# Batch 2 of a fused attention and MLP kernel put in the order of the later batches, and the loads and transposes of batches 3 and 4 moved to other places and queues

## The chip, the cores and the metric

The kernel runs on one core of one Trainium2 chip. The metric is the device time of one execution in microseconds (us); a lower time is better. A core has five engines that run side by side, each with its own queue of instructions in order: TensorE (PE in the profile; PEld are its weight loads), VectorE (DVE), ScalarE (ACT), GpSimd (POOL) and SyncE (SP), which here only issues DMAs. GpSimd issues DMAs too, between its own instructions. All share 16 DMA engines.

## The reference

Eight batches of eight heads with 576 tokens and a head width of 64 go through causal attention with a forgetting gate; the result, laid out as tokens by 512 features, goes through a two-layer MLP (512 to 2048, exact GELU, 2048 to 512). All data are given as fp32.

```
scores = scale * np.matmul(q, k.transpose(0, 1, 3, 2))
log_f = np.log(np.clip(f, 0.0001, 1.0))
cum = np.cumsum(log_f, axis=-1)
decay = cum[:, :, :, None] - cum[:, :, None, :]
scores = np.where(causal, -1000000000.0, scores + decay)
...
attn = attn / (np.sum(attn, axis=-1, keepdims=True) + 1e-09)
return np.matmul(attn, v).astype(np.float32)
...
h = x @ w_in
g = 0.5 * h * (1.0 + erf(h * inv_sqrt2))
return (g @ w_out).astype(np.float32)
```

## The kernel before

**Work of one batch.** The kernel goes through the batches one by one and writes the order of every engine's work out by hand. Heads are taken in four pairs `i`, the 576 tokens in five blocks of 128 (the last overlaps the fourth by 64). For each pair, `scores` makes four tiles `t` of transposed scores on TensorE (L319), ScalarE takes their exponential (L329), and GpSimd zeroes what lies above the diagonal with selects (L331), five for each pair. The decay of the forgetting gate is a weight on the keys: `weigh_v` multiplies v by it on GpSimd (L288) and writes the weight itself into a 65th column (L295). `attend` multiplies the exponentials with the weighted v (L350, "value products"); `divide` on VectorE divides by the 65th column (L369, L370) and leaves x. Then x has to be transposed into `xT`, which `x_dma` does with a DMA transpose from SP (L397). `gemm1` multiplies w_in with xT (L447, blocks `ffb` 0 to 15 of 128 hidden features), ScalarE applies GELU (L467), and the second product with w_out (L551 and others) gives 512 rows of the output, in four row blocks `ts`, copied and added by VectorE (L565, L575) and stored by SP (L579).

**The 64 tokens that are over.** 576 is 512 and 64. The MLP takes 512 tokens of each batch at a time; the last 64 tokens of all eight batches are collected in `tails` and go through the MLP together at the end. In batches 1 and 3 to 7, `attend` takes four query blocks, `tail` computes the 64 tokens for all heads in one go (L416), and `tail_end` transposes them into `tails` by DMA (L429). In batches 0 and 2, `blocks(b)` gives five blocks; in batch 2 the fifth block of xT is copied into `tails` by GpSimd (`x_tail`, L435) once xT is there.

**The filling.** While ScalarE works on a batch's exponentials, TensorE does the second product of the batch before: `take(fill, n)` puts n steps of it behind each score tile. A step marked "r" is two matmuls on 64 rows each, which write into two PSUM banks that VectorE adds up later (scores also use 64 rows); a step "n" is one matmul on 128 rows. `PLAN` is the order of the four row blocks with the PSUM pool ("o", "m" or "s") that holds each. Batch 2 has more to fill in: the second half of two row blocks of batch 0 (`gemm2_second`, 16 steps), the other two of batch 0 (`PLAN_0`, 32) and all of batch 1 (`PLAN_1`, 64); a later batch has the 64 of its predecessor.

**Order in batches 3 to 7** (`attention`). All score tiles with their filling; then the value products of pairs 0 to 3 (`av`, and `av_both` for pairs 1 and 2 together in a PSUM bank pair of scores), the tail between fills, the rest of the filling, and `gemm1_open`, which starts seven blocks of the first product in step with the arrival of x. VectorE then untangles q and k of the next batch (L269), sixteen copies for q and sixteen for k, and GpSimd weighs the next v.

**Order in batch 2.** The value products of pair i−1 come in the middle of the score tiles of pair i, with a divide and an x transpose each; those of the last pair come behind all scores. The first product has an opening of its own.

**What is loaded when.** There is one buffer for v (`v_sb`), one for the weighted v, and one for the transposed q and k (`tq_of`); q and k as loaded have two. So v of a batch can be loaded when the weighing of the batch before is over, and q, k can be transposed (`transpose_dma`, in two halves of four heads, L255) when the batch before is untangled. In batches 3 to 7 SP issues: the first half of q, k of the next batch, v of the next batch, the second half, and later x. In batch 2, SP issues x of pair 0, then v of batch 3 (L134) and the first half of q, k of batch 3, then x of the other pairs, and the second half behind them. GpSimd issues the load of q, k of batch b+2 (L120) among the weighings of batch b+1, at block 14 of the first product (block 9 in batch 1).

**A tile that is used twice.** x has four buffers; `tail_end` takes one of them as the fifth of a batch, so its divide waits until the x transpose of pair 0 is over. `behind` (L641) is a small GpSimd copy that makes GpSimd's queue wait until a tile is there; here it is used once, in batch 1.

Of the kernel before, what the change touches and what calls it, by code (L numbers as in the profile page):

```python
# [54 lines left out]
def kernel(  # L55
# [18 lines left out]
    XC = NBLK * P  # L74
    TL = S - TC
    assert B * TL == TC
# [281 lines left out]
    def normalize(b, i, h):  # L358
        if (b, i) not in x_of:
            x_of[b, i] = x_pool.tile([P, NBLK, 2, D], BF16, tag="x", name="x")  # L360
        nm = blocks(b)
        divide(x_of[b, i][:, 0:nm, h, :], o_of[b, i, h], nm)

    def blocks(b):
        return NBLK if b in (0, 2) else NBLK - 1
# [11 lines left out]
    def xT(b):  # L377
        if b not in xT_of:
            xT_of[b] = xT_pool.tile([P, n_dm, XC], BF16, tag="xT", name="xT")
        return xT_of[b]  # L380

    def to_xT(b, i, copy, pool=m_psum, tag="m", ps=None):
        if ps is None:
            shape = [P, 2, 1024] if pool is s_psum else [P, XC]
            ps = pool.tile(shape, BF16, tag=tag, name="ps_x")
            if pool is s_psum:
                ps = ps[:, 0, 0:XC]
        nm = blocks(b)
        for m in range(nm):
# [3 lines left out]
        copy(xT(b)[:, i, 0 : nm * P], ps[:, 0 : nm * P])  # L393

    def x_dma(b, i):
        nm = blocks(b)
        nc.sync.dma_start_transpose(  # L397
            xT(b)[:, i, 0 : nm * P].rearrange("d (m p) -> d m p", p=P),
            x_of[b, i][:, 0:nm].rearrange("p m h d -> p (m h d)"),
# [25 lines left out]
    def tail_end(b, o):  # L425
        x = x_pool.tile([P, NBLK, 2, D], BF16, tag="x", name="x")
        x = x.rearrange("p k h d -> p (k h) d")[:, 0:HP]
# [5 lines left out]

    def x_tail(b):
        nc.gpsimd.tensor_copy(tails[:, :, b], by_half(xT(b)[:, :, XC - TL :]))  # L435

# [40 lines left out]
    def gemm2(c):  # L477
# [43 lines left out]
    PLAN_0 = [(2, "o", 16 * "r"), (3, "m", 14 * "r" + 2 * "n")]  # L521
    PLAN_1 = [
        (0, "m", 14 * "r" + 2 * "n"),
        (1, "m", 14 * "r" + 2 * "n"),
        (2, "m", 12 * "r" + 4 * "n"),
        (3, "s", 16 * "n"),
    ]
# [3 lines left out]
    def gemm2_rows(c, plan):  # L531
# [4 lines left out]
        for ts, held, steps in plan:  # L536
            if held == "s":
                both = s_psum.tile([P, 2, d_model], FP32, tag="s", name="ps2")
                banks = [both[:, 0], both[:, 1]]
            else:  # L540
                pool = {"o": o_psum, "m": m_psum}[held]
                banks = [
                    pool.tile([P, d_model], FP32, tag=held, name="ps2")
                    for _ in range(2)
                ]
            ot = o_pool.tile([P, d_model], FP32, tag="ot", name="ot")
            for kt, step in enumerate(steps):
                last = kt == steps.rfind("r")
                for r in range(2 if step == "r" else 1):
# [5 lines left out]
                        start=kt == (steps.index("r") if r else 0),  # L555
# [546 lines left out]
```

## Time and profile before

| | |
|---|---|
| median of 3 runs | 330.33 us |
| lowest and highest | 328.84 and 330.5 us |
| profiled execution | 330.98 us |
| its span, first to last instruction | 329.3 us |
| TensorE, VectorE, ScalarE, GpSimd busy | 317.3, 179.6, 203.1, 131.2 us |
| DMA mean | 133 GB/s |
| first product, matmuls (L447) | 112.8 us, 379 ns mean of one |
| second product while filling (L551) | 104.4 us |

The span is a little shorter than the execution's time because what lies before the first and behind the last instruction is not in it. A matmul's own duration (379 ns) is longer than its share of the time, since matmuls overlap; a chain or a stretch tells better what a row of them takes. A timeline row has the start, the duration, the engine and line, the operation, what it writes and reads, the shape and the count; in brackets the idle time before it and what ended it. DMAs have two times: that of the issuing instruction on its queue, and that from the issue to the landing of the data.

### The profile page before, as it was taken

How to read it: one execution, taken by the hardware profiler on the slowest of the kernel's cores; microseconds unless marked ns; L12 is line 12 of the kernel's file. 1: busy time of each engine (PE TensorE's matmuls, PEld its weight loads, DVE VectorE, ACT ScalarE, POOL GpSimd, SP SyncE). 2: the span in 40 equal slices, each digit the busy share in tenths (PEclk: the TensorE clock that was granted, in tenths of full speed). 3: DMA queues.
4: the chain of work that ended last, by engine and by line, in shares of the span. 5: the costliest groups of instructions: out<-in, count | busy, mean ns of one | idle time of the engine just before them, and what ended most of it. 6: DMA issues, size and time to landing. Idle time of an engine off the chain costs nothing.

```text
span 329.3 us, 8075 instructions
## 1 busy us (share of the span) xinstructions
PE 317.3 (96%) x3291; PEld 168.9 (51%) x3323; DVE 179.6 (55%) x424; ACT 203.1 (62%) x296; POOL 131.2 (40%) x254
## 2 busy tenths in 40 slices
PE   7999799999999999999999999999999999999995
PEld 3664445445554456445644565455545564444443
DVE  5852566584458935792599449953795270010011
ACT  4896785984635797189808990899178936405600
POOL 8996883019426153804471356225512510000000
PEclk9999999999999999999999999999999999999999
DMA  7999999988998999499959794969610131021012
GB/s 114 190 192 211 207 189 124 185 176 144 196 220 180 146 201 199 74 158 170 218 76 175 141 222 95 176 120 202 129 41 3 66 82 56 0 88 42 0 47 83
DMA packets 94117, 43.93 MB, mean 133 GB/s; under 512 B 73344, under 2 KB 88960, under 8 KB 94080
## 3 DMA queue, kind: packets, MB, share of 16 engines
q1 hardware_dynamic: 76928, 26.90, 41.1%
q0 software_dynamic: 16752, 15.99, 30.8%
q8 instruction: 26, 0.43, 0.6%
q10 hardware_dynamic: 400, 0.52, 0.4%
q14 instruction: 11, 0.09, 0.1%
HBM read 36.85 MB, written 9.44 MB: 141 GB/s over the span
## 4 chain that ended last, share of the span: by engine, by line
PE 84%; DMA 9%; POOL 3%; issue 1%; ACT 1%; DVE 0%; another core or an unknown queue 0%; POOLq 0%; DVEq 0%
PE ps L447 35%; PE ps L551 26%; PE ps L491 8%; PE s L319 6%; PE o L350 5%; DMA q<-in_k_dram 3%; DMA k<-in_k_dram 3%; DMA v_sb<-in_v_dram 2%; DMA xT<-x 1%; PE o L416 1%; PE ps L615 1%; ACT e L329 1%; POOL q L120 1%; POOL k L120 1%; POOL v_sb L169 1%
## 5 line engine op out<-in xcount | busy, mean ns | idle before, releaser
L467 ACT ACTIVATE g<-ps 128x512 bf16<-128x512 f32 x138 | 75.8, 616 | 85.5 <-PE ps L447 84.4
L447 PE MATMUL ps<-xT,w_in_sb 128*128 128x512 bf16 x498 | 112.8, 379 | 1.9 <-remote 0.3
L551 PE MATMUL ps<-w_out_sb,g 64*128 64x512 bf16 (+1 forms) x737 | 104.4, 376 | 0.8 <-issue 0.5
L329 ACT ACTIVATE e<-s 128x896 bf16<-128x896 f32 x112 | 87.8, 836 | 15.3 <-PE s L319 13.8
L447 PEld LDWEIGHTS <-w_in_sb 128*128 128x128 bf16 x576 | 55.0, 98 | 67.1 <-issue 3.2
L331 POOL TENSOR_SCALAR_AFFINE_SELECT e<-e 128x256 bf16<-128x256 bf16 (+1 forms) x135 | 49.2, 386 | 86.5 <-ACT e L329 86.4
L551 PEld LDWEIGHTS <-g 64*128 64x128 bf16 (+1 forms) x751 | 42.1, 94 | 31.3 <-issue 1.3
L288 POOL TENSOR_TENSOR vw<-v_sb,wT 128x640 bf16<-128x640 f32 (+1 forms) x30 | 38.1, 1272 | 34.7 <-DMA v_sb<-in_v_dram 18.6
L269 DVE COPY qT<-tq 64x288 bf16<-64x288 bf16 x96 | 43.0, 448 | 2.9 <-DMA tq<-q 1.4
L565 DVE COPY ot<-ps 128x512 f32<-128x512 f32 x20 | 13.8, 692 | 54.3 <-PE ps L551 54.3
L319 PE MATMUL s<-qT,kT 64*128 64x256 bf16 (+1 forms) x336 | 37.8, 275 | 0.8 <-DVE kT L241 0.6
L269 DVE COPY kT<-tk 64x288 bf16<-64x288 bf16 x96 | 35.4, 369 | 3.8 <-DMA tk<-k 2.1
L500 DVE COPY ot<-ps 128x512 f32<-128x512 f32 (+2 forms) x9 | 5.7, 632 | 49.5 <-PE ps L491 49.5
L319 PEld LDWEIGHTS <-kT 64*128 64x128 bf16 x336 | 18.1, 94 | 19.8 <-issue 4.0
L491 PE MATMUL ps<-w_out_sb,g 128*128 128x512 bf16 (+2 forms) x142 | 27.9, 355 | 0.1
L370 DVE TENSOR_TENSOR x<-o,r 128x256 bf16<-128x256 f32 (+1 forms) x51 | 22.2, 435 | 4.9 <-DMA xT<-x 3.3
L350 PEld LDWEIGHTS <-e 128*128 128x128 bf16 x600 | 20.2, 98 | 4.6 <-issue 2.1
L350 PE MATMUL o<-vw,e 128*128 128x65 bf16 x600 | 21.4, 194 | 0.2 <-POOL e L331 0.2
L491 PEld LDWEIGHTS <-g 128*128 128x128 bf16 x144 | 13.5, 98 | 14.5
L575 DVE TENSOR_TENSOR ot<-ot,ps 128x512 f32<-128x512 f32 x27 | 18.6, 688 | 3.0 <-remote 0.7
L447 PE MATMUL ps<-tails,w_in_sb 128*128 128x512 bf16 x64 | 14.3, 378 | 0.0
L670 ACT ACTIVATE e<-s 128x1024 bf16<-128x1024 f32 (+1 forms) x13 | 12.1, 990 | 2.1 <-PE s L665 1.9
(92 smaller groups left out, 192.0 us busy)
## 6 DMA issues: line engine op xcount, KB each, us to landing
out_dram<-ot SPq DMA_DIRECT2D x32, 256.0 KB, 2.7
v_sb<-in_v_dram SPq DMA_DIRECT2D x24, 256.0 KB, 4.8
q<-in_q_dram POOLq DMA_DIRECT2D x6, 576.0 KB, 7.0
k<-in_k_dram POOLq DMA_DIRECT2D x6, 576.0 KB, 9.5
v_sb<-in_v_dram POOLq DMA_DIRECT2D x17, 128.0 KB, 6.3
w_in_sb<-in_moe_w_in_dram POOLq DMA_DIRECT2D x4, 512.0 KB, 8.3
w_out_sb<-in_moe_w_out_dram POOLq DMA_DIRECT2D x4, 512.0 KB, 8.5
v_sb<-in_v_dram SPq DMA_DIRECT2D x6, 128.0 KB, 4.6
```

Source lines behind the costliest of these rows:

```text
L269: nc.vector.tensor_copy(rows[:, odd], src[odd * D : (odd + 1) * D, 2 * i + h].rearrange("d j p -> d p j"),)
L288: eng.tensor_tensor(vw(b)[:, hs, n0:n1, 0:D], v_sb[:, hs, n0:n1, :], w.unsqueeze(3).to_broadcast([P, 2, n1 - n0, D]), Alu.mult,)
L319: nc.tensor.matmul(to, *ab, start=half < 0, stop=half == 1 or not masked)
L329: nc.scalar.activation(et[:, :, z:c], st[:, :, z:c], Act.Exp, scale=scale)
L331: nc.gpsimd.affine_select(out=et[:, :, c0 + z : c0 + P], in_=et[:, :, c0 + z : c0 + P], compare_op=Alu.is_ge, fill=0.0, base=z, pattern=[[ ...
L350: nc.tensor.matmul(o[:, m, :], e_of[b, i, t][:, h, c : c + P], vw_of[b][:, 2 * i + h, n, :], start=(n == 0), stop=(n == m),)
L370: nc.vector.tensor_tensor(x, o[:, 0:n, 0:D], r[:, 0:n].unsqueeze(2).to_broadcast([P, n, D]), Alu.mult,)
L447: nc.tensor.matmul(ps, w_in_sb[:, kt, ffb * P : (ffb + 1) * P], xT(c)[:, kt, 0:TC] if c < B else tails[:, kt % 2, :, kt // 2, :], start=(k ...
L467: nc.scalar.activation(g_of[c][ffb], ps, Act.Gelu)
L491: nc.tensor.matmul(pss[ts][:, c0:c1], g_of[c][kt][:, ts * P : (ts + 1) * P], w_out_sb[:, kt, c0:c1], start=(kt == 0), stop=(kt == n_ff - 1),)
L551: nc.tensor.matmul(banks[r], g_of[c][kt][rows, ts * P : (ts + 1) * P], w_out_sb[rows, kt, :], start=kt == (steps.index("r") if r else 0), ...
L575: nc.vector.tensor_tensor(ot, ot, bank, Alu.add)
```

## The change

Batch 2 goes through the same code as batches 3 to 7: four query blocks, all scores first, value products behind them, a tail, `gemm1_open`. `PLAN_1` and its special cases go, `PLAN_0` has 16 steps "r" in its second row block, and the counts of the filling for batch 2 change so that 101 of the 112 steps lie between its score tiles. `tail_end` has a tile of its own (tag "xt"), and xT shrinks from 640 to 512 columns. Both halves of q, k of batch 3 are transposed in the middle of batch 2's scores, ahead of every x. Behind the opening of batch 2's first product, GpSimd waits for the x of pair 3 (`behind`), loads v of batch 3, then q and k of batch 4, and only then weighs v of batch 3. In the batches behind it, `behind` stands in front of the load of q and k. The cut diff:

```diff
     def normalize(b, i, h):
...
-        nm = blocks(b)
-        divide(x_of[b, i][:, 0:nm, h, :], o_of[b, i, h], nm)
-
-    def blocks(b):
-        return NBLK if b in (0, 2) else NBLK - 1
+        divide(x_of[b, i][:, 0:NQ, h, :], o_of[b, i, h], NQ)
...
     def tail_end(b, o):
-        x = x_pool.tile([P, NBLK, 2, D], BF16, tag="x", name="x")
-        x = x.rearrange("p k h d -> p (k h) d")[:, 0:HP]
+        x = x_pool.tile([P, HP, D], BF16, tag="xt", name="xt")
...
-    def x_tail(b):
-        nc.gpsimd.tensor_copy(tails[:, :, b], by_half(xT(b)[:, :, XC - TL :]))
...
-    PLAN_0 = [(2, "o", 16 * "r"), (3, "m", 14 * "r" + 2 * "n")]
-    PLAN_1 = [
-        (0, "m", 14 * "r" + 2 * "n"),
-        (1, "m", 14 * "r" + 2 * "n"),
-        (2, "m", 12 * "r" + 4 * "n"),
-        (3, "s", 16 * "n"),
-    ]
+    PLAN_0 = [(2, "o", 16 * "r"), (3, "m", 16 * "r")]
...
         yield from gemm2_rows(0, PLAN_0)
-        yield from gemm2_rows(1, PLAN_1)
+        yield from gemm2_rows(1, PLAN)
...
-    FILL_2 = [[8, 8, 8, 8], [8, 8, 4, 4], [4, 4, 4, 4], [4, 4, 4, 4]]
+    FILL_2 = [[8, 8, 8, 8], [8, 8, 8, 7], [5, 5, 5, 5], [5, 5, 6, 2]]
...
         for i in range(HP):
             for t in range(4):
                 scores(b, i, t)
                 take(fill, counts[i][t])
-                if t == 1 and b == 2 and i > 0:
-                    av(i - 1)
-                    if i == 1:
-                        load_v(3)
...
-                if b > 2 and i == 0 and t == 1:
+                if b > 2 and (i, t) == (0, 1):
                     load_v(b + 1)
-                if b > 2 and t == 0 and i < 2:
-                    transpose_dma(b + 1, 4 * i, 4 * i + 4)
-                if b == 2 and t == 1 and i == 1:
-                    transpose_dma(3, 0, 4)
+                for half, at in enumerate([(2, 0), (2, 2)] if b == 2 else [(0, 0), (1, 0)]):
+                    if (i, t) == at:
+                        transpose_dma(b + 1, 4 * half, 4 * half + 4)
+        av(0)
+        av_both(b, 1)
+        av_both(b, 2)
+        av(3)
+        take(fill, 4)
+        tail_end(b, tail(b))
+        put_off.pop()()
+        take(fill, 999)
+        gemm1_open(b)
         if b == 2:
-            take(fill, 4)
-            transpose_dma(3, 4, 8)
-        take(fill, 999)
...
+            behind(xT(b), HP - 1)
+            load_v(b + 1, eng=nc.gpsimd)
+            load_qk_tokens(b + 2)
         if b + 1 < B:
             untangle(b + 1, 0)
             weigh_v(b + 1, 0)
-        if b == 2:
-            x_tail(b)
...
+                if ffb == (10 if b == 1 else 14) and b != 2 and b + 2 < B:
+                    if b > 2:
+                        behind(xT(b), HP - 1)
+                    load_qk_tokens(b + 2)
...
-                if ffb == (9 if b == 1 else 14):
-                    load_qk_tokens(b + 2)
```

## The prediction

> **What bounds the kernel now.** The first part of the page and the chain that ended last say it together.
>
> ```profile
> PE 317.3 (96%) x3291; PEld 168.9 (51%) x3323; DVE 179.6 (55%) x424; ACT 203.1 (62%) x296; POOL 131.2 (40%) x254
> PE 84%; DMA 9%; POOL 3%; issue 1%; ACT 1%; DVE 0%; another core or an unknown queue 0%; POOLq 0%; DVEq 0%
> ```
>
> TensorE is busy 96% of the span and is 84% of the chain; the DMA share lies in the first 45 us, before batch 2. So an edit pays only by taking work or gaps from TensorE. Next I cut the span into one stretch per batch, from its first score matmul to the next batch's (view of stretches; columns: length, then busy us and count of PE, PEld, DVE, ACT, POOL).
>
> ```profile
> 67.86:113.31 45.45, 44.87 (x427) 22.71 (x432) 30.08 (x66) 25.11 (x35) 22.24 (x41) 1.00 1.04 182
> 113.31:147.67 34.36, 33.91 (x347) 18.34 (x349) 23.25 (x56) 23.46 (x34) 14.69 (x30) 1.00 0.84 153
> 147.67:181.67 34.00, 33.84 (x347) 18.49 (x349) 23.56 (x54) 23.46 (x34) 14.76 (x30) 1.00 0.91 154
> ```
>
> Batch 2 takes 45.45 us, batch 4 takes 34.00, batch 3 34.36; the granted clock is 1.00 in all. Batch 2 is longer because it carries 112 filling steps of the second product (16 left of batch 0, 32, and 64 of batch 1) where a later batch carries 64. A step's price is in the chain view: 16 row-half matmuls of L551, eight steps, take 1.73 us, so 0.216 each. The 48 extra steps are 10.37 us, and batch 2 in a later batch's order should take 34.00 + 10.37 = 44.37 us. It takes 1.08 more. The PE timeline of batch 2 shows where.
>
> ```profile
> 79.16 0.38 PE L551 MATMUL ps<-w_out_sb,g 128*128 128x512 bf16 x1 [0.16 <-issue]
> 79.37 1.12 PE L350 MATMUL o<-vw,e 128*128 128x65 bf16 x30
> 80.42 0.36 PE L319 MATMUL s<-qT,kT 64*128 64x448 bf16 x2
> ```
>
> Between the row-half matmuls (64*128) and scores, each of three pairs' value products is cut in as full-height matmuls (128*128), with 0.16 us idle on the way in, at 79.16, 84.45 and 89.75.
>
> **TensorE's part, step by step.** (1) Value products go from five to four query blocks: 15 to 10 matmuls per head, 40 fewer; 30 take 0.95 us in the chain, so −1.27. (2) The tail is added: 40 matmuls of L416, 0.77 in batches 3 to 7. Net −0.50. (3) The three cut-ins go: −0.48 of shown idle. (4) The rest, 0.10, is the small loss on the way back to scores. The sum is −1.08, the same as the difference above. Steps "n" turned into "r" cost nothing: 35 full-height matmuls of L491 take 7.55 us, 0.216 each, a pair of row halves the same. The denser filling (8, then 5 steps between score tiles) leaves ScalarE more room than later batches' 3: five steps and a tile are 1.25 us, an exponential 0.84 (L329).
>
> **VectorE and PSUM.** Batch 2's 16 divides of five blocks (0.19 + 0.49) become those of batch 3 (eight of 0.18 + 0.42 turned partly into two pairs of 0.20 + 0.69, and a tail of 0.17 + 0.42), at the same or less work. An additional copy for the last row block (0.69) is hidden: VectorE waited 11.2 us for L551's matmuls in this batch. The o banks before the first value product are free in time by batch 3's row: copy ends 0.7 us and addition 1.5 us after the row block, while 1.2 us of matmuls and 0.33 of the first head lie between.
>
> **SP: v leaves, transposes move up.** Before, SP issues x of pair 0 at 81.93 (6.5 us to landing), then v of batch 3 for 7.13 us, and the second transposes (100.87 and 102.23) after x. Now the stores stay, the two q/k halves come in front of all x. They need k of batch 3: issued 76.28, landing 11.6 later, 87.9, with v and x beside it; less without. They take 1.3 to 2.2 us of SP each, so SP ends them near 93, and the third and fourth stores come behind (0.5 each). Value products start at 67.86 + (127.68 − 113.31) + 10.37 = 92.6; x of pair 0 is divided 1.7 later, 94.3. SP is free by then by under 1 us. I take 0 to 0.3 for this. The fifth transposition (tails by DMA, 1.2 us of SP at 135.68 in batch 3) replaces a GpSimd copy of 0.43 that waited 4.9 us for x; nobody needs tails until the end.
>
> **GpSimd and the DMA behind x.** x of pair 3 is issued 21.07 us after batch 3's start and lands 2.3 later; in batch 2 that is 67.86 + 10.37 + 23.4 = 101.6. Then the gate copy (0.19, row L641), five v issues (L134, 0.75 each: 3.75) and q, k (0.8 each) until 107.1. The last v issue, near 105, lands 4.3 to 6.9 later (POOL's v issues at 12.3 and 33.4; the second had other loads in front): 109 to 112, I take 110. The four weighings (1.28 + 0.27 each) then end near 116; before, they ended at 108. Behind them on GpSimd are batch 3's 20 selects (7.7 us). The next batch starts at 112.3, its value products at 126.7, the last at 128.7. So v may land as late as 128.7 − 6.2 − 7.7 = 114.8 before TensorE feels it: hidden, by 5 us. If that cover went, each us costs one. q, k of batch 4 are issued about when they were (104.98 before) and land near 115; in batches over 2 their gate waits for x of pair 3, which lands at 136.7 where q was issued at 136.35: 0.5 later, hidden by SP's wait for VectorE (transposes at 147.70).
>
> What is late next is the untangling on VectorE. These rows of batch 2 are of VectorE and of GpSimd:
>
> ```profile
> 101.47 3.53 DVE L269 COPY kT<-tk 64x288 bf16<-64x288 bf16 x4
> 102.02 1.33 POOL L288 TENSOR_TENSOR vw<-v_sb,wT 128x640 bf16<-128x640 f32 x1
> 105.03 3.37 DVE L269 COPY qT<-tq 64x288 bf16<-64x288 bf16 x4
> 105.79 0.77 POOL L120 DMA_DIRECT2D k<-in_k_dram  x1
> ```
>
> Four copies take 1.35 us alone and 3.5 beside GpSimd. From 102.02 to 108.1 VectorE lost 4.2 us to 6.1 us of GpSimd. Now GpSimd works 5.4 us issuing and 6.2 weighing under the same copies: about 7.5 lost at that row's two thirds (ends: nothing, and all 11.6). They start at 99.1 and end near 117.4, 5.1 us into batch 3 (1.9 before). First needed is pair 1 at +4.6, done by 110. But SP's transposes for batch 4 wait for these copies (113.93 after the last q copy), then load v (4.75), then the second half, two stores, and x of pair 0, issued 16.2 us into the batch. I reckon SP 0.9 us late there.
>
> ```profile
> 129.55 6.04 SPq L397 DMA_TRANSPOSE xT<-x x4
> 133.75 13.99 PE L447 MATMUL ps<-xT,w_in_sb 128*128 128x512 bf16 x63 [0.34 <-remote]
> ```
>
> In batch 3 that x took 4.1 us to land, and TensorE waited 0.34; in batch 4 it took 2.3 and nothing waited. SP late by 0.9 makes the wait 0 to 1.5; I take 0.6, 0.3 more than now.
>
> The load of q, k of batch 3, moved from block 9 to 10 of batch 1's first product, keeps its place on GpSimd between the weighings: nothing. The tail's own tile takes away VectorE's wait for x (3.3 us in three batches). TensorE did not wait for it: nothing.
>
> **Sum.** −1.1 + 0.1 (x in batch 2) + 0.3 = −0.7. The profiled execution took 330.98 us (span 329.3, 1.7 around it); it would become 330.3. The median of the runs, 330.33, is 0.65 lower, so I forecast 329.6.
>
> **A rule that speaks against it.** The row: q, k issued by GpSimd amid the copies took 0.82 and 0.77, as at 75.45 without copies (0.84, 0.77); VectorE's copies were what grew. The Trainium skill, "SBUF — State Buffer", section "SBUF: two separate sides", says that a VectorE copy in a two-port mode locks GpSimd out, so that descriptors of its DMAs can't be written; it names about 620 ns becoming 3100. By the row nothing is added; by the page's figure seven issues would last some 22 us, and v would come past its deadline.
>
> **Rivals.**
> (A) Forecast, 0.52: 329.6, own range 328.9 to 330.6.
> (B) All waits for x vanish in batches 2 and 3: −1.1 − 0.34, 328.9. For it: batch 4's 2.3 us. 0.18.
> (C) Slower: the chain GpSimd, VectorE copies, SP. x of pair 0 in batch 3 has 3.86 us from issue to need (129.55 to 133.41), against 2.3 to 4.1 of landing. Once SP is over 1.5 us late, each further us is TensorE's; at 4.5 late, with a landing of 2.3 to 3.2, it pays 3 to 3.9, net about +2: 332.3. For it: two thirds of the copies' slowdown is an estimate. Against: load v can wait less. 0.20.
> (D) GpSimd locked out until the copies end at 110: v's issues from 110 to 114, landing 118 to 121, weighings and selects 13.9 more: 132 to 135 against 128.7, and batch 4's transposes behind them: some 5 us, 335. This is what the page's rule would do; the row speaks against it. 0.05.
> (E) The transposes don't get in front as meant, because k of batch 3 lands late: x of batch 2 waits behind them by 1 us and takes the gain: 330.3. Against it: 87.9. 0.05.
>
> The range 328.6 to 332.0 leaves out D and most of C's end. Faster by over 0.5% (about what a measurement of this kernel can tell from no change; below 328.7): half of B and the low edge of A, 0.12. Slower (above 332): over half of C, and D, 0.17. Between: 0.71.
>
> **What would show it.** Right: batch 2 from first score to next near 44.4 us, no 0.16 idles inside; v landing by 112; weighings under the start of batch 3; first-product wait in batch 3 under 1 us. Wrong: a batch 3 over 35 us with an x landing as releaser, selects late at the value products, or a wait of L551 for a bank.

## The result and the profile after

| | before | after |
|---|---|---|
| median of 21 runs each | 330.11 us | 331.49 us |
| lowest and highest | 328.84 and 334.07 us | 330.43 and 334.54 us |
| ratio after to before, 95% interval | | 1.0051 [1.0028, 1.0075] |
| profiled execution, span | 330.98, 329.3 us | 332.16, 330.4 us |

The changed kernel is slower by about half a per cent. The forecast, 329.6, was a small gain. The time lies inside the range, on the side of rival C, but it moved the other way than was forecast.

These lines of the page of the changed kernel answer to the first two of before: busy time by engine, and the chain that ended last.

```profile
PE 321.0 (97%) x3338; PEld 169.8 (51%) x3338; DVE 178.8 (54%) x423; ACT 202.7 (61%) x296; POOL 136.6 (41%) x262
PE 91%; DMA 4%; DVE 2%; issue 1%; ACT 1%; POOL 1%; SPq 0%; POOLq 0%; DVEq 0%
```

They tell little: TensorE is still nearly always busy, with 3.7 us more of it, though the change gives it no more to do. Most of this is the record: the first profile of the kernel before has 3291 matmuls for 3323 weight loads, so 32 matmuls are missing from it, while a second profile (below) has all 3323 and 320.0 us. The 1.0 us that is left may go with the granted clock, which shows 0.6 in the second of the page's 40 slices, 8 to 16 us in, where the kernel before had 0.9 or more. The stretches by batch say more. The rows are batches 2, 3, 4, and batch 7 with the end (start and end, length, then busy us and count of PE, PEld, DVE, ACT, POOL, the granted clock, DMA share, GB/s).

```profile
68.12:112.58 44.46, 44.46 (x446) 22.14 (x446) 28.80 (x68) 24.58 (x35) 20.92 (x38) 1.00 0.84 168
112.58:148.34 35.76, 34.22 (x350) 18.40 (x351) 23.65 (x54) 23.47 (x34) 20.30 (x39) 1.00 0.91 165
148.34:182.34 34.00, 34.00 (x350) 18.49 (x350) 22.24 (x50) 23.47 (x34) 15.01 (x31) 1.00 0.81 153
250.34:330.40 80.06, 76.04 (x558) 38.12 (x557) 15.85 (x33) 33.62 (x51) 7.33 (x20) 1.00 0.16 48
```

The row of before for batch 7 and the end, not shown so far, is this one:

```profile
249.84:329.30 79.46, 75.61 (x553) 38.16 (x557) 15.96 (x33) 33.62 (x51) 7.33 (x20) 1.00 0.16 48
```

Batch 2 went from 45.45 to 44.46 us. (That all 44.46 are busy is no sign of a closed gap: in the second profile of the kernel before, all of batch 2's 45.45 are busy too.) Batch 3 went from 34.36 to 35.76; its POOL column grew by 5.6 us, since the weighings of v slid into it. Batch 7 with the end grew by 0.6. With the unrounded times (the spans are 329.27 and 330.45), from the first scores on: −0.98 (batch 2), +1.39 (batch 3), −0.17 (batch 6), +0.67 (batch 7 and end), in all +0.91; what lies before batch 2 adds 0.26. That is the difference between the spans. (What lies before batch 2 scattered by some 2 us between the profiles; from batch 2 on, the two of the kernel before agree within 0.02 us in every stretch, see below.)

**Batch 2** gained what was forecast. Its PE timeline where the value products come in, behind the last scores:

```profile
92.22 0.59 PE L530 MATMUL ps<-w_out_sb,g 64*128 64x512 bf16 x4
92.75 2.78 PE L350 MATMUL o<-vw,e 128*128 128x65 bf16 x80
95.37 1.02 PE L530 MATMUL ps<-w_out_sb,g 128*128 128x512 bf16 x4
96.32 0.84 PE L410 MATMUL o<-vw,e 128*64 128x65 bf16 x40
97.10 1.68 PE L530 MATMUL ps<-w_out_sb,g 128*128 128x512 bf16 x7
98.68 2.53 PE L437 MATMUL ps<-xT,w_in_sb 128*128 128x512 bf16 x11
```

The value products are one row of 80, then filling, the tail, filling, and the first product, whose x is there. No row carries an idle time in brackets. But the 0.16 that stood at each cut-in in the first profile of the kernel before were missing records and no idle time: the second profile has 14 matmuls in a row there, where the first has 12, a gap and 1.

```profile
76.88 2.00 PE L551 MATMUL ps<-w_out_sb,g 64*128 64x512 bf16 x14
78.72 1.12 PE L350 MATMUL o<-vw,e 128*128 128x65 bf16 x30
```

**Batch 3** pays. Its first product waits for x, 1.54 us. Before, it was 0.34 by the first profile, in which the matmul ahead of the wait is missing, and 0.13 by the second, which has it; the difference of 1.41 is all that batch 3 lost (1.39).

```profile
134.43 2.75 PE L437 MATMUL ps<-xT,w_in_sb 128*128 128x512 bf16 x12 [1.54 <-DMA xT<-x]
```

To see why that x is late, follow its queue, SP, back (timeline of SP; start and duration of the issue, not the landing):

```profile
115.29 1.28 SPq L255 DMA_TRANSPOSE tq<-q  x1
118.22 1.25 SPq L255 DMA_TRANSPOSE tk<-k  x1
119.57 4.80 SPq L134 DMA_DIRECT2D v_sb<-in_v_dram  x5
...
125.94 1.33 SPq L255 DMA_TRANSPOSE tq<-q  x1
127.33 1.62 SPq L255 DMA_TRANSPOSE tk<-k  x1
129.05 1.41 SPq L554 DMA_DIRECT2D out_dram<-ot  x2
130.65 6.45 SPq L391 DMA_TRANSPOSE xT<-x  x4
```

From 118.22 to 130.65 SP has hardly a gap. The kernel before in the same place:

```profile
115.40 1.50 SPq L255 DMA_TRANSPOSE tk<-k  x1
117.00 4.75 SPq L134 DMA_DIRECT2D v_sb<-in_v_dram  x5
...
125.97 2.23 SPq L579 DMA_DIRECT2D out_dram<-ot  x2
```

There the last store ends at 128.20 and x follows at 129.55: SP had 1.35 us to spare, until VectorE had divided x, 16.2 us into the batch. Counted from the batch's start, the transposition of k is issued at 5.64 instead of 2.09, 3.55 later; 1.35 of that is the spare time, 0.37 SP's shorter row of issues, and 1.83 is left: x is issued at 18.07 instead of 16.24. It lands 3.65 later and not 4.06, and TensorE needs it 20.31 into the batch: 18.07 + 3.65 − 20.31 = 1.41, and 0.13 from the landing to the matmul.

And why is k transposed late? Because it lands late, at 118.17, 0.05 before that issue. The timeline of GpSimd behind batch 2's first product:

```profile
101.83 0.34 POOL L616 CAST gate<-xT 96x1 f32<-96x1 bf16 x1 [8.17 <-DMA xT<-x]
102.35 4.56 POOL L134 DMA_DIRECT2D v_sb<-in_v_dram  x5 [0.19 <-issue]
106.91 0.85 POOL L120 DMA_DIRECT2D q<-in_q_dram  x1
107.75 0.86 POOL L120 DMA_DIRECT2D k<-in_k_dram  x1
113.16 1.28 POOL L288 TENSOR_TENSOR vw<-v_sb,wT 128x640 bf16<-128x640 f32 x1 [4.55 <-DMA v_sb<-in_v_dram]
```

The gate opens at 101.83, when x of pair 3 is there. The five v issues take 4.56 us, and v is complete at 113.0, 10.6 us after the first issue (the weighing at 113.16 waited for it). q and k stand behind v in the same queue: k, issued at 107.75, lands 10.4 us later, where before it took 8.6 from 105.79. VectorE is not what holds SP here; its untangling, from the first of these rows to the last, is over at 111.82:

```profile
99.42 1.33 DVE L269 COPY qT<-tq 64x288 bf16<-64x288 bf16 x4
...
110.48 1.34 DVE L269 COPY kT<-tk 64x288 bf16<-64x288 bf16 x4
```

### The profile page after: what moved, and what is told of

Same layout as the page of the kernel before. It is cut to its first block, busy times and chain, and to the rows that moved or that the text cites. A ratio compares the mean times of both kernels' runs of the same rounds, so it can differ in the third digit from the quotient of the medians.

```text
span 330.4 us, 8131 instructions
## 1 busy us (share of the span) xinstructions
PE 321.0 (97%) x3338; PEld 169.8 (51%) x3338; DVE 178.8 (54%) x423; ACT 202.7 (61%) x296; POOL 136.6 (41%) x262
## 4 chain that ended last, share of the span: by engine, by line
PE 91%; DMA 4%; DVE 2%; issue 1%; ACT 1%; POOL 1%; SPq 0%; POOLq 0%; DVEq 0%
PE ps L437 38%; PE ps L530 26%; PE ps L481 8%; PE s L319 6%; PE o L350 4%; DMA xT<-x 2%; PE s L640 2%; DMA q<-in_q_dram 2%; PE ps_f L226 1%; PE o L410 1%; PE ps L590 1%; ACT e L329 1%; PE o L671 1%; PE ps L566 1%; DVE x L366 0%
## 5 line engine op out<-in xcount | busy, mean ns | idle before, releaser
L530 PE MATMUL ps<-w_out_sb,g 64*128 64x512 bf16 (+1 forms) x766 | 107.1, 376 | 0.0
L269 DVE COPY qT<-tq 64x288 bf16<-64x288 bf16 x96 | 39.4, 410 | 2.5 <-DMA tq<-q 1.0
L269 DVE COPY kT<-tk 64x288 bf16<-64x288 bf16 x96 | 37.9, 394 | 3.6 <-DMA tk<-k 1.9
L550 DVE TENSOR_TENSOR ot<-ot,ps 128x512 f32<-128x512 f32 x28 | 19.3, 688 | 4.1 <-PE ps L530 2.1
L481 PEld LDWEIGHTS <-g 128*128 128x128 bf16 x144 | 13.5, 98 | 14.5
L350 PEld LDWEIGHTS <-e 128*128 128x128 bf16 x560 | 18.6, 98 | 3.9 <-issue 2.1
L350 PE MATMUL o<-vw,e 128*128 128x65 bf16 x560 | 19.7, 194 | 0.2 <-POOL e L331 0.2
L366 DVE TENSOR_TENSOR x<-o,r 128x256 bf16<-128x256 f32 x41 | 17.4, 424 | 1.4
```

Source lines behind the costliest of these rows:

```text
L269: nc.vector.tensor_copy(rows[:, odd], src[odd * D : (odd + 1) * D, 2 * i + h].rearrange("d j p -> d p j"),)
L350: nc.tensor.matmul(o[:, m, :], e_of[b, i, t][:, h, c : c + P], vw_of[b][:, 2 * i + h, n, :], start=(n == 0), stop=(n == m),)
L366: nc.vector.tensor_tensor(x, o[:, 0:n, 0:D], r[:, 0:n].unsqueeze(2).to_broadcast([P, n, D]), Alu.mult,)
L481: nc.tensor.matmul(pss[ts][:, c0:c1], g_of[c][kt][:, ts * P : (ts + 1) * P], w_out_sb[:, kt, c0:c1], start=(kt == 0), stop=(kt == n_ff - 1),)
L530: nc.tensor.matmul(banks[r], g_of[c][kt][rows, ts * P : (ts + 1) * P], w_out_sb[rows, kt, :], start=kt == 0, stop=last if r else kt == n_f ...
L550: nc.vector.tensor_tensor(ot, ot, bank, Alu.add)
```

## The experiments

The theory from these profiles: GpSimd's queue has v ahead of q and k of batch 4, so k lands late, SP's list of batch 4's transposes and loads starts late, and x of batch 3 stands at the end of that list. Rivals: the load of v of batch 4, which waits for the late weighings, is what holds SP; the order of batch 2's work is at fault by itself, or the moved loads by themselves; the gate (L616) holds GpSimd for nothing; the wait was a chance of that one execution. In the diffs, "-" is the changed kernel unless said otherwise. Ratios are to the kernel before.

**v of batch 3 earlier.** GpSimd loads it as soon as its buffer is free, amid batch 2's scores.

```diff
                     weigh_v(b, 3)
+                    load_v(3, eng=nc.gpsimd)
...
-            load_v(b + 1, eng=nc.gpsimd)
```

> v of batch 3 is loaded by GpSimd right behind the weighing of batch 2's v, about 20 us earlier; behind x only q, k of batch 4 are loaded. Theory S (the changed kernel loses in batch 3 because k of batch 4, queued behind v on GpSimd, lands at 118.2 where it landed at 114.4, so that SP transposes it late, loads v late and issues x of pair 0 late): k lands near 112, the wait before batch 3's first product falls from 1.5 us to 0.4 or less, batch 2 keeps its 44.5 us, and the whole is 1.0 us (0.6 to 1.6) faster than the kernel before. Rival G (the loss lies in the gates of the later batches or in the last batch): batch 3's wait goes, but the whole stays at or above the kernel before. Rival X (v now runs beside q, k of batch 3, which land later, and their transposes push x of batch 2): a wait of 1 us or more before batch 2's first product.

Measured: 1.0095 [1.006, 1.0131]. Batch 3 is mended, 34.76 us: k of batch 4 lands at 113.55, x of pair 0 is issued 16.25 us into batch 3, the wait is 0.54. But batch 2 takes 47.30. In the first row, from SP's timeline, a transpose of batch 3's first half lasts 4.35 us beside v's transfer; the second, from PE's, is TensorE's wait in batch 2, for an x that was issued only at 96.60 and landed at 99.68. (The row names a VectorE copy as releaser, but that is the last of several, long done.)

```profile
87.26 4.35 SPq L255 DMA_TRANSPOSE tk<-k  x1
```

```profile
99.81 13.97 PE L437 MATMUL ps<-xT,w_in_sb 128*128 128x512 bf16 x64 [2.73 <-DVE kT L269]
```

So the late v is the cause of batch 3's wait, and early v collides with the transposes that the change put in front of x.

**q, k of batch 4 ahead of v of batch 3** in GpSimd's queue.

```diff
-            load_v(b + 1, eng=nc.gpsimd)
             load_qk_tokens(b + 2)
+            load_v(b + 1, eng=nc.gpsimd)
```

> Behind x, GpSimd loads q, k of batch 4 first and v of batch 3 second. Theory S: k lands near 111, so the first transposes of batch 4 are on time, but v lands near 117 instead of 113, the weighing ends near 123 instead of 118.7, and SP, whose load of the next v waits for the weighing, is late by as much or more: the wait before batch 3's first product stays at 1.5 us or grows to 4, the whole is 0 to 2.5 us slower than the changed kernel. A rival by which only the landing of k counts: the wait falls to 0.4 or less and the whole comes to 1 us under the kernel before. A rival by which v's lateness reaches TensorE itself through the selects: a wait of the value products of batch 3 for GpSimd's selects or weighings.

Measured: 1.0149 [1.0114, 1.0184]. k lands at 111.62, as the theory wants, but v only at 116.23, and the weighings last to 122. Now v decides twice: selects behind the weighings come late for the value products, and SP's load of v of batch 4 waits for the weighings, to 121.97, so x is issued 20.85 us into the batch. Timeline of PE in batch 3:

```profile
128.50 1.00 PE L350 MATMUL o<-vw,e 128*128 128x65 bf16 x18 [0.61 <-POOL e L331]
...
135.18 5.12 PE L437 MATMUL ps<-xT,w_in_sb 128*128 128x512 bf16 x23 [2.42 <-DMA xT<-x]
```

The order in which the change issues them is the better one: what is too much behind the gate is the sum of both loads. In the changed kernel, too, v stands close behind k as a cause. The last of its weighing multiplications ends at 118.57, 1.0 us before SP, held by k, comes to the load of v of batch 4 (119.57), so a k on time would by itself have won back about 1 us of SP's time at most.

**v of batch 4 by ScalarE**, to take the load of 4.8 us out of SP's list.

```diff
-                if b > 2 and (i, t) == (0, 1):
+                if b > 3 and (i, t) == (0, 1):
                     load_v(b + 1)
+                if b == 3 and (i, t) == (2, 0):
+                    load_v(b + 1, eng=nc.scalar)
```

> The loads stay as in the changed kernel, but in batch 3 the five loads of batch 4's v are issued by ScalarE behind the scores of pair 2 instead of by SP. Theory S (SP's queue is what is late): SP issues x of pair 0 near 128.3 instead of 130.65, the wait before the first product of batch 3 falls from 1.5 to 0.4 us or less, the whole is 0.7 to 1.2 us faster than the kernel before. Rival D (the transfers themselves are late, not SP): x is issued on time and still lands past 133, the wait stays over 1 us. Rival A (ScalarE's five issues delay its exponentials): TensorE waits for exponentials in batch 3 by up to 3 us.

Measured: 1.0287 [1.0239, 1.0334]. The five issues held ScalarE for 7.76 us, the exponentials behind them came late, and TensorE waited 6.77 us in the midst of the scores (timeline of ScalarE):

```profile
119.73 7.76 ACTq L134 DMA_DIRECT2D v_sb<-in_v_dram  x5
127.54 2.21 ACT L329 ACTIVATE e<-s 128x768 bf16<-128x768 f32 x3 [7.25 <-DMA v_sb<-in_v_dram]
```

Within that wait the granted clock fell to 0.5, from 126.3 to 133.2, which adds to the time. The run says nothing on SP, because a larger wait lies in front of it.

**No gate** ahead of v.

```diff
-            behind(xT(b), HP - 1)
             load_v(b + 1, eng=nc.gpsimd)
```

> In batch 2 GpSimd no longer waits for x of pair 3 before it loads v of batch 3 and q, k of batch 4: v is issued from 94 on instead of 102. Theory S: v lands near 103, k of batch 4 near 110, the wait in batch 3 falls to 0.4 or less, and the whole is 0.5 to 1.2 us faster than the kernel before, less what x of batch 2 loses. Rival X (x shares the DMA engines with v): x of batch 2 lands 1 to 3 us later and the wait moves into batch 2, so the whole stays where the changed kernel is.

Measured: 1.0207 [1.0165, 1.0249]. Batch 3 is at 34.74 with a wait of 0.52, but batch 2 takes 52.31: v, issued from 92.6 on, runs beside the x transposes, which then land at 100.0, 104.6, 107.4 and 109.8, and the first product stands still four times (2.52, 1.79, 0.94 and 0.74 us). The first two, in the timeline of PE:

```profile
100.13 2.72 PE L437 MATMUL ps<-xT,w_in_sb 128*128 128x512 bf16 x6 [2.52 <-DMA xT<-x]
104.64 1.89 PE L437 MATMUL ps<-xT,w_in_sb 128*128 128x512 bf16 x8 [1.79 <-DMA xT<-x]
```

These waits are 5.99 of the 7.84 us that batch 2 takes longer than in the changed kernel; part of the rest is the granted clock, 0.5 from 99.7 to 103.1. The gate earns far more than it costs.

**The order of the work alone**: batch 2 in the new order, every load and transpose where it was before (cut; "-" is the changed kernel).

```diff
-            behind(xT(b), HP - 1)
-            load_v(b + 1, eng=nc.gpsimd)
-            load_qk_tokens(b + 2)
...
+                if b == 2 and (i, t) == (1, 1):
+                    load_v(3)
+                    transpose_dma(3, 0, 4)
...
         put_off.pop()()
+        if b == 2:
+            transpose_dma(3, 4, 8)
```

> One half of the change alone: batch 2 in the order of the later batches, but v of batch 3 and the first half of q, k of batch 3 issued by SP in the middle of batch 2's scores as in the kernel before, the second half behind x, and q, k of batch 4 loaded at block 14 behind three weighings. Theory S (the order is worth 1 us, the moved loads take it back in batch 3): batch 2 takes 44.4 to 45.1 us, batch 3 34.0 to 34.5, the whole is 0.5 to 1.2 us faster than the kernel before. Rival X (v and the transposes on SP make x of batch 2 late, which is what the moved loads were for): a wait of 1 to 3 us before batch 2's first product, and a whole at or above the kernel before.

**The loads and transposes alone**: batch 2 in the old order, with v by GpSimd, the gate and the transposes as in the change (cut; "-" is the kernel before).

```diff
-                    if i == 1:
-                        load_v(3)
...
-                if b == 2 and t == 1 and i == 1:
-                    transpose_dma(3, 0, 4)
+                if b == 2 and i == 2 and t in (0, 2):
+                    transpose_dma(3, 2 * t, 2 * t + 4)
...
-            transpose_dma(3, 4, 8)
...
+            behind(xT(b), HP - 1)
+            load_v(3, eng=nc.gpsimd)
+            load_qk_tokens(4)
```

> The other half alone: batch 2 in its old order, with both transposes of q, k of batch 3 in the middle of the scores, and GpSimd loading v of batch 3 and then q, k of batch 4 behind x of pair 3, ahead of weighing. Theory S: batch 2 keeps 45.4 us, batch 3 has the changed kernel's wait of 1 to 2 us before its first product, the whole is 0.8 to 1.8 us slower than the kernel before. Rival O (the loss comes with the new order, not with the loads): batch 3 near 34.4 us and the whole within 0.4 us of the kernel before.

Measured: order alone 1.0152 [1.0112, 1.0193], loads alone 1.0011 [0.9985, 1.0038]. Neither half is the change. With the order alone, TensorE already waits 1.24 us for x before batch 2's first product, and the second transposes of batch 3 come behind an x that is now issued as late as 93.98, run into the load of q, k of batch 4, and k's lasts 5.93 us; tq of batch 4 follows at 118.38, x is issued 20.88 us into batch 3, and TensorE waits 3.85. Timeline of SP, order alone:

```profile
103.76 5.93 SPq L255 DMA_TRANSPOSE tk<-k  x1
...
118.38 1.29 SPq L255 DMA_TRANSPOSE tq<-q  x1
```

So the change needs its moved transposes to be worth anything. With the loads alone the wait of x in batch 3 is 0.53 with the same record missing as in the first profile of the kernel before (0.34 there), and the reason is time. Here are the gate and v in GpSimd's timeline:

```profile
99.59 0.18 POOL L641 CAST gate<-xT 96x1 f32<-96x1 bf16 x1 [6.39 <-DMA xT<-x]
100.10 4.66 POOL L134 DMA_DIRECT2D v_sb<-in_v_dram  x5 [0.33 <-issue]
```

Batch 3 starts at 112.84 in this kernel, at 112.58 in the changed one. In the old order x of pair 3 lands 13.3 us ahead of that start, in the new one 10.8, because all value products, the tail and the filling stand between the scores and the first product, and the four transposes come in one go. The whole row of loads behind the gate slides 2.5 us into batch 3, and SP, which has 1.35 us to spare there, cannot take it.

**q, k of batch 3 earlier** as well (loaded from block 5 of batch 1, transposed one pair earlier, batch 2's weighings together in batch 1, v of batch 3 behind them; cut).

```diff
-                for half, at in enumerate([(2, 0), (2, 2)] if b == 2 else [(0, 0), (1, 0)]):
+                for half, at in enumerate([(1, 0), (1, 2)] if b == 2 else [(0, 0), (1, 0)]):
...
-                if ffb == (10 if b == 1 else 14) and b != 2 and b + 2 < B:
+                if ffb == (5 if b == 1 else 14) and b != 2 and b + 2 < B:
...
+                if b == 1 and ffb == 15:
+                    load_v(3, eng=nc.gpsimd)
```

> The changed kernel with the DMA queue filled where it was idle (72 to 77 us): q, k of batch 3 are loaded by GpSimd as soon as k of batch 2 is transposed, in front of the weighing of batch 2, so 10 us earlier; they are transposed in batch 2's second pair; all four weighings of batch 2 come together, and v of batch 3 is loaded right behind them, 10 us ahead of x. Behind x only q, k of batch 4 are loaded. Theory S: x of batch 2 is undisturbed, k of batch 4 lands near 112, batch 2 takes 44.4 to 44.8 us and batch 3 34.0 to 34.5; the whole is 0.7 to 1.3 us faster than the kernel before. Rival Q (the DMA engines have no room left, each earlier load only pushes another): v of batch 2 lands late by several us and the wait shows up in batch 2, or x of batch 2 is late by over 1 us as in the run with v loaded early.

Measured: 1.0095 [1.0062, 1.0127]. Batch 2's own v came late (77.9 instead of 72) and its value products waited 0.61 for selects; k of batch 4 lands early, at 111.6, but the weighings ran beside VectorE's untangling, and SP's first transpose waited for that. x was issued 16.47 us into batch 3, took 4.69 to land, and TensorE waited 1.20, or about 1.0 with the matmul whose record is missing there. Batches 2 and 3 took 45.83 and 35.21.

**The kernel before, once more**, to see what one profile is worth.

> The kernel before once more, for a second profile: which parts of the sum of stretches are its own scatter. Batches 0 and 1 took 61.2 us to the first score of batch 2 in the first profile, batch 2 45.45, batch 3 34.36, batch 7 and the end 79.4; I expect batch 3 to 6 within 0.4 of that, and can't say for the rest.

Measured: 330.29 us. Batches 2 to 7 take 45.45, 34.38, 34.00, 34.00, 34.15 and 79.41 us; in the first profile 45.45, 34.37, 34.00, 34.00, 34.17 and 79.43. Only what lies before batch 2 differs (60.6 and 61.2 us from batch 0's first score). This profile lacks no matmul. Its rows for batches 2 and 3:

```profile
67.20:112.65 45.45, 45.45 (x431) 22.72 (x431) 29.43 (x63) 25.11 (x35) 22.21 (x41) 1.00 1.00 179
112.65:147.03 34.38, 34.25 (x350) 18.32 (x350) 23.36 (x57) 23.46 (x34) 14.63 (x30) 1.00 0.84 152
```

Not every profile is so quiet. In six of the variants (v of batch 4 by ScalarE, each half alone, the gate at pair 1, v around its transfer, four loads more) TensorE waits some 4.5 us into batch 2 for VectorE's additions, and 0.35 to 0.75 us are lost there. In all but v around its transfer that is ahead of anything their edits do, so it doesn't count against them.

**v of batch 3 not loaded at all.** Batch 3 then works with batch 2's v, so its part of the output is another one.

```diff
-            load_v(b + 1, eng=nc.gpsimd)
```

> The changed kernel without the load of batch 3's v (batch 3 then uses batch 2's v, so its part of the output is another one): the load of q, k of batch 4 follows the wait for x at once. Theory S (behind x, v and q, k stand in one row, and the second in it is late for SP): k of batch 4 lands near 111, SP is on time, batch 3 takes 34.0 to 34.6, batch 2 keeps 44.4, the whole is 0.6 to 1.4 us faster than the kernel before. Rival: the weighing, now early, slows VectorE's untangling as in the kernel before and its transposes wait for that instead: batch 3 keeps 0.5 us or more of its 1.5 us of waiting. Rival G (other costs of the change, such as the gates in later batches): a whole at or above the kernel before although batch 3 is repaired.

Measured: 0.999 [0.9962, 1.0018]. Batch 2 keeps its gain (44.42) and batch 3 falls from 35.76 to 34.73, with a wait of 0.52. SP in batch 3:

```profile
115.78 1.32 SPq L255 DMA_TRANSPOSE tk<-k  x1
117.19 4.73 SPq L134 DMA_DIRECT2D v_sb<-in_v_dram  x5
...
128.12 5.77 SPq L391 DMA_TRANSPOSE xT<-x  x4
```

k lands at 111.65 instead of 118.17, its transposition is issued 4.16 us into the batch instead of 5.64, and x at 16.51. Here it is VectorE that releases the transposes, since the weighings run beside its copies (four of them took 7.27 us there, 1.34 alone). This prices the load of v behind the gate: 1.03 us of TensorE's time, as much as batch 2 gains.

**The gate at pair 1** instead of pair 3, a middle between gate and none.

```diff
-            behind(xT(b), HP - 1)
+            behind(xT(b), 1)
```

> The changed kernel with GpSimd waiting in batch 2 for x of pair 1 instead of pair 3, so v and q, k are issued some 2.6 us earlier. Theory S: k of batch 4 lands 2 to 2.6 us earlier, and batch 3's wait falls from 1.5 to about 0.5 us; x of pairs 2 and 3 now runs beside v and lands 0 to 2 us later, of which the first product of batch 2 feels up to 1 us. The whole lies between 0.5 us under and 0.5 us above the changed kernel. If x suffers as it did without any gate, batch 2 takes 2 us or more longer and the whole is slower than the changed kernel by that.

Measured: 0.9995 [0.996, 1.003]. The profiled execution, 332.73 us, is 2.2 above the median of its runs (330.51) and shows waits of 0.41 in batch 2 and 2.18 in batch 3, with k of batch 4 landing as late as in the changed kernel (117.86): it was issued 3.4 us earlier and took 13.5 us instead of 10.4. The profile speaks for a wait no smaller than the changed kernel's, the median for a small gain on it; inconclusive.

**v of batch 3 early, and the transposes put around its transfer** (as with q, k of batch 3 earlier, but with the halves at (1, 2) and (2, 0), and the load of q, k of batch 3 behind the landing of batch 2's v; cut).

```diff
-                for half, at in enumerate([(2, 0), (2, 2)] if b == 2 else [(0, 0), (1, 0)]):
+                for half, at in enumerate([(1, 2), (2, 0)] if b == 2 else [(0, 0), (1, 0)]):
...
+                        behind(v_sb[:, :, 2, :], H - 1)
...
+                if b == 1 and ffb == 15:
+                    load_v(3, eng=nc.gpsimd)
```

> The changed kernel with loads moved to where the DMA engines were idle, without getting in v of batch 2's way: GpSimd issues q, k of batch 3 when the third load of batch 2's v has landed (near 70 us), weighs all four pairs of batch 2 together, and loads v of batch 3 behind them, near 79 us; the transposes of batch 3 come a little earlier; behind x only q, k of batch 4. Theory S: v of batch 3 lands before 90, x of batch 2 is undisturbed, k of batch 4 lands near 112, and the whole is 0.3 to 1.2 us faster than the kernel before. Rival Q (no room on the DMA engines): x of batch 2 lands late again, by 1 us or more. Rival V (the weighing of batch 3 beside VectorE's untangling makes the next transposes late): batch 2 near 44.4 us, and a wait of 1 us or more before batch 3's first product.

Measured: 1.0029 [0.9993, 1.0065]. In the profile, the fastest of its runs (329.33, 2.3 under the median), batch 3 waits for nothing (34.25) while batch 2 keeps hardly anything of its gain: 45.42, with waits of 0.25 for VectorE's additions (0.42 lost there) and 0.33 for x. Not faster than the kernel before.

**Four small loads more on SP.** Batch 7's wait is in no list of causes so far. x of pair 0 of the changed kernel lands there 4.3 us after its issue; the median of the four pairs is 2.9. The kernel before has 122 DMAs on SP, the changed one 118.

```diff
+                if (b, i, t) == (2, 1, 0):
+                    for k in range(4):
+                        extra = x_pool.tile([BH, 16], FP32, tag="extra", name="extra")
+                        nc.sync.dma_start(extra, f.rearrange("b h s -> (b h) s")[:, 0:16])
```

> Four more small loads (64 rows by 16 values each), read by nobody, are issued by SP in batch 2, behind pair 0's scores, where SP has time; nothing else of the changed kernel is different. It asks two things. (1) Is the wait of TensorE in batch 3 the same in another execution? By the theory that q, k of batch 4 land late behind v (Q), k of batch 4 lands near 118 again, x of pair 0 is issued some 18 us into batch 3, and the wait is 1.2 to 1.9 us, batch 3 near 35.8. By the rival that the first look at the changed kernel was a chance of that execution, the wait comes back under 0.8. (2) Does the late landing of the x transpose in front of batch 7's first product (3.1 us behind the issue's end instead of 1.1 to 1.2) hang on how many DMAs SP has issued before it? If it does, it moves to another transpose, four places earlier, and batch 7's wait of 0.24 us goes; if it hangs on something else (time, or the instructions of other engines), it stays at x of pair 0 in batch 7. The time: that of the changed kernel within 0.3 us, ratio to before 1.003 to 1.007.

Measured: 1.0022 [0.9992, 1.0052]. Batch 3, and batch 7 with the end:

```profile
111.08:148.22 37.14, 34.23 (x351) 18.45 (x351) 23.59 (x54) 23.47 (x34) 20.26 (x39) 1.00 0.97 168
250.29:329.70 79.41, 75.88 (x558) 38.19 (x557) 15.79 (x33) 33.62 (x51) 7.29 (x20) 1.00 0.17 48
```

Batch 3's wait is there again, and larger, 2.91 us: k lands 6.1 us into the batch (5.6 in the changed kernel), the load of v takes SP 5.73 us, and x is issued at 20.07. So the wait was no chance of one execution, but its size is not the same in each; this is over the 1.9 that was expected. It can hardly be as large in most executions of this program, whose median is 0.7 us under that of the changed kernel; there is one profile of each. Batch 7 with the end is back at the length of the kernel before. These are the first products of batch 7, first of the changed kernel, then of this one:

```profile
270.83 2.53 PE L437 MATMUL ps<-xT,w_in_sb 128*128 128x512 bf16 x11 [0.24 <-DMA xT<-x]
```

```profile
270.38 2.97 PE L437 MATMUL ps<-xT,w_in_sb 128*128 128x512 bf16 x13
```

What is late moved from x of pair 0 to x of pair 1, where nobody waits for it: not four places earlier, as expected, but one later, just where the kernel before has it. Of the 0.67 us that batch 7 with the end lost, 0.40 lie ahead of its first product, 0.27 behind the last matmul (3.83 us to the end of the span, 3.55 before); both are gone here (20.09 us to the first product, 3.55 at the end). So the 0.5 us that batches 6 and 7 lost together hang on SP's list, and not on anything that the change does there.

## Why the prediction was wrong

- **TensorE's part in batch 2** (−1.08, to 44.37): right in size, −0.98 and 44.47. Step (3) read missing records as 0.48 of idle time; the second profile of the kernel before shows none. What both profiles show at the first cut-in is 1.83 or 1.84 us from the start of the filling to the value products, where eight steps take 1.73, and 1.04 or 1.05 to the next score, where 30 value products of the new row take 0.98. Three times 0.17 is 0.5, close to steps (3) and (4) together (0.58), so the sum held by some luck.
- **x in batch 2** (+0.1): SP was free in time, x of pair 0 was issued at 94.61 (94.3 was forecast) and cost nothing.
- **GpSimd and v**: the gate at 101.8 was forecast as 101.6. "0.75 each" for the v issues was 0.96 for four of the five; the 0.75 came from loads of 128 KB, and these four are of 256 KB. The last v landed at 113.0, not 110, and the weighings ended at 118.7, not 116. TensorE did not feel that directly, as forecast: 1.8 us of the 5 of cover were left.
- **The step that failed** is "q, k of batch 4 are issued about when they were (104.98 before) and land near 115". They were issued 1.9 later and landed at 115.24 and 118.17, because v, 10.6 us long, stood ahead of them in the same queue. The landing was near that of the kernel before (114.36), where nothing stood there. Without v, k landed at 111.65 and 1.03 us came back. What followed is the sign that the prediction named: a batch 3 over 35 us (35.76) with an x landing as releaser.
- **VectorE's untangling** ("end near 117.4") was wrong the other way: it ended at 111.82. Eight groups of 1.35 are 10.8 us alone, and they took 12.4: GpSimd's issues cost the copies 1.6 us, not the 7.5 that were drawn from a row beside weighings (two thirds of the 11.6 would be 7.7). The weighings that slow the copies had not begun, for v was late.
- **SP** ("0.9 us late"): 1.83. The forecast's own 5.1 − 1.9 = 3.2 for the start of the row, less the 1.35 us that SP has to spare before x, would have given 1.85. So the start of the row was nearly right by luck, from a wrong cause, and the subtraction was not made. The wait that followed, 1.54, is the upper end that the prediction named (1.5), where it took 0.6. The "0.34" that it started from was 0.13 and a missing record.
- **What no step had**: the late landing in batch 7 and the longer end, +0.67, less 0.17 in batch 6.
- **The rule that was weighed**, the Trainium skill's "SBUF — State Buffer", section "SBUF: two separate sides" (a VectorE copy in a two-port mode starves GpSimd's descriptors, 620 becoming 3100 ns): no issue here grew in that way. Beside the copies, four issues took 0.96 us each and the fifth, of half the size, 0.76; with v of batch 3 loaded earlier, beside no row of copies, they took 0.90 to 0.95 and 0.72. Whether these copies are in such a mode no run shows. Rival D did not come.

Rival C came about: the chain that ends at SP's x. Its first link was the queue of GpSimd's DMAs, not VectorE, and it was worth 1.4 us and not 3. Together with batch 7 that was enough to turn −1.0 into a loss. No variant that was run beats the kernel before: five (0.999, without v; 0.9995; 1.0011; 1.0022; 1.0029) have 1 in their intervals, the others are slower.

## What to carry to other kernels

A load that is moved to another queue has to be followed through everything behind it on that queue: price each landing with the new neighbours in front, not by where it landed before. Before a stage is closed up, write down how much spare time each DMA queue has there before its next hard deadline (here SP: 1.35 us), because a saving on the main engine also brings that deadline nearer to the landings that feed it. A change in two halves can be worth less or more than either; run each half alone. Before an idle time of a fraction of a matmul is put into a sum, count the matmuls against the weight loads, or take a second profile.

## What was not expected of the hardware

**A landing that is late by the list.** SP's x transposes mostly land 1.1 to 1.2 us after the end of their issue. From batch 4 on, about one in each batch takes 2.1 to 3.3 us, or an issue is stretched from 1.2 to about 2 us. In batch 7, which one it is goes with the number of DMAs on SP: in both profiles of the kernel before and in the one with four loads more (122 each) it is x of pair 1, the 109th DMA; in the changed kernel and all seven variants with 118 it is x of pair 0, the 104th. The other lists fit: with 117 (the loads alone) it is the 104th again, now x of pair 1; with 123 (the order alone) the 109th, now x of pair 0; with 113 (v of batch 4 by ScalarE) x of pair 0, the 99th, and the one behind it. In earlier batches the place varies among programs with the same number. What makes it late is open.

**The same five issues cost their engine very different times.** The load of v took GpSimd 4.3 to 4.7 us, SP 4.1 to 8.0 (7.13 in batch 2 of the kernel before), and ScalarE, in its one run, 7.8. Whether the issuer or what else is in transfer makes the difference was not tried.

**Transfers stretch transposes.** A transposition of k that took SP 1.25 us with no load in transfer (118.22 in the changed kernel) took 4.35 beside v's transfer and 5.93 beside q's and k's.
